# Two experts' second weights in column halves instead of three, and five batches with their left output half first instead of six

## Chip, cores, metric

One core of a Trainium2 chip runs the whole kernel. The metric is the device time of one execution in microseconds; the kernel before takes 181.04 us, the median of three runs (180.8 to 181.2).

## What is computed

Attention over 8 batches, 8 heads, 576 positions of 64 values (a sliding window of 32 for four heads, a dilated one for the other four), followed by a soft mixture of eight experts with four slots each. The change lies in the second part. With `x` the attention output as 4608 rows of 512:

```python
logits = x @ phi                                  # 4608 x 32
d = exp(logits - logits.max(0)); d /= d.sum(0)    # over the rows
slot_input = (d.T @ x).reshape(8, 4, 512)
for e in range(8):
    h = np.maximum(slot_input[e] @ w1[e], 0.0)    # 4 x 1024
    slot_out[e] = h @ w2[e]                       # 4 x 512
c = exp(logits - logits.max(1)); c /= c.sum(1)    # over the slots
return c @ slot_out.reshape(32, 512)              # 4608 x 512, float32
```

Every weight is read once: `w1` and `w2` have 2 MB for each expert in float32, and are held in float16 (1 MB).

## The kernel before

The attention is a software pipeline over the eight batches, in an order of steps written out by hand (`ORDER`, `STEPS`); the whole program is scheduled in the order in which it is written. All large transfers are issued by POOL, the inputs and weights (which are cast to float16 on the way) as well as the output, and so stand in one order. POOL issues the inputs of each batch, then the `w1` of the experts between them, then the `w2` of 0 to 2 (`load_w2`, L202).

Once the last inputs are consumed, their memory is released and takes the `w2` of experts 3 to 7 (L555 to L566). Experts 3 and 4 come whole, one transfer each of 8 KB per partition (L205). Experts 5, 6 and 7 come in column halves: first the left 256 output columns of 5, 6 and 7, then the right ones. A half is two transfers (L211, `u` 0 and 1), each of four rows of 256 columns per partition, so four transfers make an expert; the prediction calls such a transfer a quarter.

After the attention, PE computes the first layer for all experts (L616), the result is transposed into `hTm`, and `emit_so(s, experts)` (L641) multiplies with `w2` for the column half `s`, accumulating all eight experts in `so[s]`, one PSUM bank for each half. `gather_so` (L658) brings a half to SBUF as float16, `spread_so` (L662) sums its four row groups and copies the sum to all of them, in `so_sb`.

`emit_batch(b, c0, c1)` (L689) makes 512 output rows for the columns `c0` to `c1`: four times `emit_fin` (L670), a matmul into one of four PSUM buffers and a scaling by ACT (L681) or DVE (L685) in turn, and then one store by POOL (L692). A store of 256 columns has 512 KB, one of 512 columns 1 MB. The last 64 rows of each batch go through `om_l` and two stores at the end (L721).

The order at the end is thus: left half of the experts' product, the left half of the output of batches 0 to 5 (`NHALF`), with the right half of the experts 5, 6 and 7 multiplied ahead of batches 2, 3 and 5; then gather and spread of the right half, the right half of the output of batches 0 to 5, batches 6 and 7 whole, and the rest rows. PE, ACT, DVE and POOL each follow this order; the semaphores between them are set by which tile an instruction reads or writes. A store needs the scalings of its batch; the quarter that an `emit_so` reads must have landed.

Of the kernel before, what the change touches and what calls it, by code (L numbers as in the profile page):

```python
# [95 lines left out]
def kernel(  # L96
# [55 lines left out]
    def slab_weights(e, tag, n):  # L152
        t = fix.tile([128, n], FP16, name=f"w2_{e}", tag=tag)
        w2t[e] = t[:, 0 : 8 * DMODEL].rearrange("p (c n) -> p c n", c=8)
# [47 lines left out]
    def load_w2(e, s=None):  # L202
        src = moe_w2[e].rearrange("(p c) n -> p c n", p=128)
        if s is None:
            nc.gpsimd.dma_start(  # L205
                out=w2t[e].rearrange("p c n -> p (c n)"), in_=src.rearrange("p c n -> p (c n)")
            )
            return
        cols = slice(DH * s, DH * s + DH)
        for u in range(2):  # L210
            nc.gpsimd.dma_start(out=w2t[e][:, 4 * u : 4 * u + 4, cols], in_=src[:, 4 * u : 4 * u + 4, cols])  # L211
# [284 lines left out]
    def step(op, b):  # L496
        if op[0] in "ARM" and op[1:] in TILES:
            kind, i = TILES[op[1:]]
            if op[0] == "A":
                tmp[(op[1:], b)] = emit_av(b, kind, i)  # L500
            elif op[0] == "R":
                tmp[("R" + op[1:], b)] = emit_recip(b, kind, i, tmp[(op[1:], b)])
            else:
                engine = nc.scalar if op[1:] in ON_ACT else nc.vector
                norm_mult(b, kind, i, tmp.pop((op[1:], b)), tmp.pop(("R" + op[1:], b)), engine)
        elif op in ("S0", "S1", "S2"):
            tmp[(op, b)] = emit_scores(b, int(op[1]))
        elif op in ("E0", "E1", "E2"):
            emit_exp(b, int(op[1]), tmp.pop(("S" + op[1], b)))
        elif op in ("MK0", "MK1", "MK2"):  # L510
            emit_mask(b, int(op[2]))
        elif op[0:2] in ("QT", "KT", "VT"):
            turn(op[0], b, int(op[2]))
        elif op in ("XP0", "XP1"):
            tmp[(op, b)] = xT_plain(b, int(op[2]))
        elif op in ("XD0", "XD1"):
            tmp[(op, b)] = xT_dil(b, int(op[2]))
        elif op in ("XPc0", "XPc1", "XDc0", "XDc1"):
            xT_copy(b, op[1], int(op[3]), tmp.pop((op[0:2] + op[3], b)))
        elif op in ("VA", "VB", "VC", "VD"):  # L520
            tmp[(op, b)] = v_rows(b, "ABCD".index(op[1]))
        elif op in ("VAc", "VBc", "VCc", "VDc"):
            v_place(b, "ABCD".index(op[1]), tmp.pop((op[0:2], b)))
        elif op in ("LG", "EP"):
            tmp[(op, b)] = (back_logits if op == "LG" else back_erow)(b)
        elif op == "ET":
            back_et(b, tmp.pop(("LG", b)))
        elif op == "ER":
            back_er(b, tmp.pop(("EP", b)))
        else:  # L530
            {"ED": back_erd, "U": back_u, "UT": back_add}[op](b)

    def loads(which, b):
        load_raw(which, b)
        if which == "V":
            if b > 2:
                load_weights(1)
            if b == B - 1:
                load_weights(len(weights))
# [6 lines left out]
    for it in range(B + max(s for _, s in STEPS)):  # L546
        for op, stage in STEPS:
            b = it - stage
            if not 0 <= b < B:
                continue  # L550
            step(op, b)
            if op in frees and b + 2 < B:
                loads(frees[op], b + 2)
            left.discard((op, b))
            if w2b_pool is None and not left:  # L555
                raw_pool.release()
                w2b_pool = tc.alloc_tile_pool(name="w2b", bufs=1, side="right")
                for e in (3, 4, 5):
                    w2t[e] = w2b_pool.tile([128, 8, DMODEL], FP16, name=f"w2_{e}", tag=f"w2_{e}")
                slab_weights(6, "qk0", QK_SLAB)  # L560
                slab_weights(7, "qk1", QK_SLAB)
                for e in (3, 4):
                    load_w2(e)
                for s in range(2):
                    for e in (5, 6, 7):
                        load_w2(e, s)  # L566
        if it == 0:
            nc.vector.tensor_copy(
                out=phi4, in_=phi_raw[:, :, None, :].broadcast_to([128, 4, 4, N_SLOTS])
            )  # L570
# [40 lines left out]
    for fc in range(2):  # L611
        for g in range(2):
            for dc in range(4):
                for j in range(4):
                    e = 4 * g + j
# [25 lines left out]
    def emit_so(s, experts):  # L641
        for c in range(8):
            for e in experts:
                g, j = divmod(e, 4)
                row = 32 * (j if len(experts) == 4 else c % 4)
                nc.tensor.matmul(
                    so[s][row : row + 32, :],
                    hTm[:, g, c, 32 * j : 32 * j + 32],
                    w2t[e][:, c, DH * s : DH * s + DH],
                    start=(e < 4 and c == 0),  # L650
                    stop=(e == 7 and c > 3),
                )
# [5 lines left out]
    def gather_so(s):  # L658
        for copy, c, c0 in part_cols(s):
            copy(out=so_part[:, c0 : c0 + DH // 2], in_=so[s][:, c : c + DH // 2])  # L660

    def spread_so(s):  # L662
        for copy, _, c0 in part_cols(s):
            rep = ring.tile([128, DH // 2], FP32, name=f"rep_{c0}", tag="ring")
            nc.tensor.matmul(rep, spread, so_part[:, c0 : c0 + DH // 2], start=True, stop=True)
            copy(out=so_sb[:, c0 : c0 + DH // 2], in_=rep)
# [22 lines left out]
    def emit_batch(b, c0, c1):  # L689
        for j in range(4):  # L690
            emit_fin(et_cols(b)[0], j, c0, c1, om[b][:, j, c0:c1], 4 * b + j)
        nc.gpsimd.dma_start(  # L692
            out=out[S * b : S * b + 512].rearrange("(j p) d -> p j d", p=128)[:, :, c0:c1],
            in_=om[b][:, :, c0:c1],
        )

    NHALF = 6
    for s in range(2):
        emit_so(s, (0, 1, 2, 3))
    for s in range(2):  # L700
        emit_so(s, (4,))
    for e in (5, 6, 7):
        emit_so(0, (e,))
    gather_so(0)
    spread_so(0)
    for b in range(NHALF):
        if b in (2, 3, 5):
            emit_so(1, ({2: 5, 3: 6, 5: 7}[b],))
        if b == 5:
            gather_so(1)  # L710
        emit_batch(b, 0, DH)
    spread_so(1)
    for b in range(NHALF):
        emit_batch(b, DH, DMODEL)
    for b in range(NHALF, B):
        emit_batch(b, 0, DMODEL)
# [43 lines left out]
```

## Time and profile before

| | us |
|---|---|
| median of three runs | 181.04 (180.8 to 181.2) |
| the profiled execution | 180.9 |
| its span, first to last instruction | 178.9 |
| PE busy | 128.0 (72%) |
| DVE busy | 125.7 (70%) |
| ACT busy | 122.2 (68%) |
| POOL busy | 56.2 (31%) |
| moved by DMA | 40.88 MB, mean 229 GB/s |

The profile counts the bytes as they arrive: float16 for inputs and weights, float32 for the output. So the weights and the output, at the same number of elements, count as one and two. Every instruction has its start and length, every transfer its issue, its packets and its landings: it raises its semaphore once for each of the 16 transfer engines that it is spread over. Times below are counted from the start of the span.

### The profile page before, as it was taken

What the parts mean: (1) busy time and instruction counts of PE and PEld (TensorE: products, weight loads), DVE (VectorE), ACT (ScalarE), POOL (GpSimd) and SP (SyncE); (2) the same over time, 40 slices, a digit from 0 to 9 for tenths busy, and PEclk for the clock granted to TensorE, in tenths of its full rate; (3) what the DMA queues carried; (4) which work ended last, traced back from release to release, by engine and by line L of the source; (5) the groups of instructions that cost most, each with busy time, mean ns of one, the idle gap of its engine ahead of it and who ended that gap; (6) DMA issues with size and microseconds to landing.
All of it is one profiled execution on the core that took longest, in us unless ns stands there. A gap on an engine that the chain in (4) does not pass through costs nothing.

```text
span 178.9 us, 5405 instructions
## 1 busy us (share of the span) xinstructions
PE 128.0 (72%) x2316; PEld 84.7 (47%) x2316; DVE 125.7 (70%) x274; ACT 122.2 (68%) x267; POOL 56.2 (31%) x94
## 2 busy tenths in 40 slices
PE   0026838989999999989989999988695346688100
PEld 0014525676667767657767757856434112221000
DVE  6483999999999999999999995472402016789200
ACT  6007757999999999999999999966002016698100
POOL 7544244224224223243420041111112414376400
PEclk9999999999999879999999999687669955555555
DMA  5999999999999999999999999999999999999994
GB/s 91 203 213 208 214 212 210 214 212 216 214 212 213 215 212 215 214 212 216 210 214 215 212 218 220 215 216 220 211 212 191 197 196 219 390 319 397 406 413 135
DMA packets 21448, 40.88 MB, mean 229 GB/s; under 512 B 1713, under 2 KB 14129, under 8 KB 20785
## 3 DMA queue, kind: packets, MB, share of 16 engines
q0 software_dynamic: 21280, 40.41, 114.2%
q8 instruction: 18, 0.29, 0.6%
q1 hardware_dynamic: 144, 0.14, 0.3%
q14 instruction: 6, 0.04, 0.1%
HBM read 62.07 MB, written 9.44 MB: 400 GB/s over the span
## 4 chain that ended last, share of the span: by engine, by line
DMA 52%; DVE 16%; PE 11%; ACT 9%; issue 3%; POOL 2%; POOLq 0%; DVEq 0%
DMA w<-in_moe_w_dram 36%; DMA rawV<-in_v_dram 10%; DMA rawK<-in_k_dram 6%; DVE vT L222 5%; DVE qk L222 4%; DVE p L283 3%; PE f L672 3%; ACT p L272 3%; ACT om L681 2%; PE s L263 2%; PE o_P L313 2%; PE rv L237 2%; ACT xp L337 1%; PE rp L357 1%; ACT vX L243 1%
## 5 line engine op out<-in xcount | busy, mean ns | idle before, releaser
L272 ACT ACTIVATE p<-s 128x1728 f16<-128x1728 f32 (+1 forms) x24 | 42.0, 1749 | 10.7 <-PE s L263 10.6
L263 PE MATMUL s<-qk 32*128 32x144 f16 (+2 forms) x640 | 29.2, 325 | 16.1 <-DVE qk L222 12.3
L313 PEld LDWEIGHTS <-p 128*128 128x128 f16 (+3 forms) x672 | 23.9, 101 | 14.0 <-issue 3.6
L263 PEld LDWEIGHTS <-qk 32*128 32x128 f16 x640 | 17.0, 118 | 20.4 <-DVE qk L222 12.3
L337 ACT ACTIVATE xp<-o_P,rc_P 128x64 f16<-128x64 f32 x96 | 23.8, 384 | 2.4 <-DVE rc_P L325 2.3
L283 DVE TENSOR_TENSOR p<-p,masks 128x1728 f16<-128x1728 f16 (+1 forms) x24 | 25.4, 1082 | 0.0
L243 ACT COPY vX<-rv 128x512 f16<-128x512 f16 (+1 forms) x32 | 23.5, 786 | 1.7 <-PE rv L237 1.6
L313 PE MATMUL o_P<-vX,p 128*128 128x65 f16 (+1 forms) x288 | 20.7, 210 | 1.3 <-DVE xp L341 0.3
L222 DVE STREAM_TRANSPOSE qk<-rawQ 128x576 uint32<-128x576 uint32 x16 | 18.9, 1243 | 2.7 <-DMA rawQ<-in_q_dram 2.7
L222 DVE STREAM_TRANSPOSE qk<-rawK 128x576 uint32<-128x576 uint32 x16 | 19.7, 1241 | 0.5 <-DMA rawK<-in_k_dram 0.5
L222 DVE STREAM_TRANSPOSE vT<-rawV 128x576 uint32<-128x576 uint32 x16 | 19.6, 1238 | 0.4 <-DMA rawV<-in_v_dram 0.4
L237 PE MATMUL rv<-cst,vT 128*128 128x128 f16 x160 | 17.3, 248 | 3.0 <-DVE vT L222 1.7
L211 POOL DMA_DIRECT2D w<-in_moe_w_dram x12 | 8.9, 745 | 29.1 <-DMA w<-in_moe_w_dram 24.8
L685 DVE TENSOR_SCALAR om<-f,rrow 128x256 f16<-128x256 f32 (+1 forms) x28 | 13.5, 518 | 3.9 <-PE f L672 3.1
L237 PEld LDWEIGHTS <-vT 128*128 128x128 f16 x160 | 12.0, 127 | 8.6 <-issue 4.3
L191 POOL DMA_DIRECT2D rawQ<-in_q_dram x16 | 8.9, 557 | 21.5 <-DVE rc_P L325 16.3
L681 ACT ACTIVATE om<-f,rrow 128x256 f16<-128x256 f32 (+1 forms) x28 | 12.8, 503 | 3.3 <-PE f L672 2.6
L672 PE MATMUL f<-so_sb,ET 32*128 32x256 f16 (+1 forms) x60 | 12.1, 420 | 3.7 <-ACT om L681 2.4
L692 POOL DMA_DIRECT2D out_dram<-om x14 | 10.4, 747 | 12.1 <-DVE om L685 9.4
L191 POOL DMA_DIRECT2D rawK<-in_k_dram x16 | 8.7, 548 | 17.1 <-DVE rc_P L325 14.6
L191 POOL DMA_DIRECT2D rawV<-in_v_dram x16 | 8.7, 547 | 10.8 <-DVE rc_P L325 8.0
L372 ACT COPY xT<-rp 128x576 f16<-128x576 f16 x16 | 10.5, 776 | 1.2 <-PE rp L357 1.2
(84 smaller groups left out, 197.4 us busy)
## 6 DMA issues: line engine op xcount, KB each, us to landing
w<-in_moe_w_dram POOLq DMA_DIRECT2D x13, 1024.0 KB, 21.7
out_dram<-om POOLq DMA_DIRECT2D x12, 512.0 KB, 6.2
rawQ<-in_q_dram POOLq DMA_DIRECT2D x16, 288.0 KB, 10.7
rawK<-in_k_dram POOLq DMA_DIRECT2D x16, 288.0 KB, 10.4
rawV<-in_v_dram POOLq DMA_DIRECT2D x16, 288.0 KB, 10.2
w<-in_moe_w_dram POOLq DMA_DIRECT2D x12, 256.0 KB, 16.4
out_dram<-om POOLq DMA_DIRECT2D x2, 1024.0 KB, 8.6
out_dram<-om_l POOLq DMA_DIRECT2D x2, 512.0 KB, 9.1
```

The source lines that it names most:

```text
L191: nc.gpsimd.dma_start(out=t[g::2, :], in_=src[4 * g : 4 * g + 4].rearrange("h (p j) d -> (h p) (j d)", j=PJ),)
L222: nc.vector.transpose(out=out_, in_=in_)
L237: nc.tensor.transpose(rg[:, n_t, :, c, :], rows, ident)
L243: copy(out=vX[b % 2][:, t0 : t0 + n, :, 0:D], in_=rg.rearrange("p n h c d -> p n h (c d)"))
L263: nc.tensor.matmul(sps[:, h, c0 : c0 + w], kk, qq, start=(tt == 0), stop=(tt == 1))
L272: return nc.scalar.activation(out=pt, in_=sps[:, :, 0:n], func=AF.Exp, scale=SCALE)
L283: return nc.vector.tensor_tensor(out=pt, in0=pt, in1=m, op=ALU.mult)
L313: nc.tensor.matmul(o[rows, h, :], lhs, rhs, start=(n == 0 or (kind == "L" and n < DIL)), stop=(n == len(jobs) - 1), skip_group_check=True,)
L337: nc.scalar.activation(out=dst[:, h], in_=src[:, h], func=AF.Copy, scale=rc[:, h : h + 1])
L672: nc.tensor.matmul(fp[:, 0 : c1 - c0], ET[32 * j : 32 * j + 32, m : m + 128], so_sb[32 * j : 32 * j + 32, c0:c1], start=True, stop=True,)
L681: nc.scalar.activation(out=dst, in_=fp[:, 0 : c1 - c0], func=AF.Copy, scale=rrow[:, blk : blk + 1])
L685: nc.vector.tensor_scalar(out=dst, in0=fp[:, 0 : c1 - c0], scalar1=rrow[:, blk : blk + 1], scalar2=None, op0=ALU.mult)
```

## The change

Expert 5's `w2` comes whole, behind those of 3 and 4, and only 6 and 7 come in column halves. Both halves of expert 5's product are multiplied ahead of the left halves of 6 and 7. Five batches instead of six have the left half of their output first; the right half of expert 6 is multiplied ahead of batch 2's left half, that of expert 7 ahead of batch 4's, and the gather of the right half follows it there. Batch 5 is then made whole, like 6 and 7.

```diff
-                for e in (3, 4):
+                for e in (3, 4, 5):
                     load_w2(e)
                 for s in range(2):
-                    for e in (5, 6, 7):
+                    for e in (6, 7):
                         load_w2(e, s)
...
-    NHALF = 6
-    for s in range(2):
-        emit_so(s, (0, 1, 2, 3))
-    for s in range(2):
-        emit_so(s, (4,))
-    for e in (5, 6, 7):
+    NHALF = 5
+    for experts in ((0, 1, 2, 3), (4,), (5,)):
+        for s in range(2):
+            emit_so(s, experts)
+    for e in (6, 7):
         emit_so(0, (e,))
     gather_so(0)
     spread_so(0)
     for b in range(NHALF):
-        if b in (2, 3, 5):
-            emit_so(1, ({2: 5, 3: 6, 5: 7}[b],))
-        if b == 5:
+        if b in (2, 4):
+            emit_so(1, (5 + b // 2,))
+        if b == NHALF - 1:
             gather_so(1)
         emit_batch(b, 0, DH)
     spread_so(1)
```

## The prediction

> **What bounds the kernel now.** I read the slices of the page first, since they show whether the transfers ever rest.
>
> ```profile
> DMA  5999999999999999999999999999999999999994
> GB/s 91 203 213 208 214 212 210 214 212 216 214 212 213 215 212 215 214 212 216 210 214 215 212 218 220 215 216 220 211 212 191 197 196 219 390 319 397 406 413 135
> q0 software_dynamic: 21280, 40.41, 114.2%
> ```
>
> The 16 transfer engines are busy from the first slice to the last but one. Two places stand out: 191 to 197 GB/s in slices 31 to 33, where w2 comes in halves, and 319 between 390 and 397 in slice 36, in the middle of the output. Nearly all of it goes through one queue, q0, fed by POOL. So I asked for windows (columns: window, length, busy of PE, PEld, DVE, ACT, POOL, clock, DMA share, GB/s).
>
> ```profile
> 112.00:132.00 20.00, 16.68 (x294) 11.90 (x290) 8.10 (x31) 10.47 (x28) 2.97 (x4) 0.68 1.03 216
> 137.00:150.00 13.00, 6.90 (x126) 3.73 (x126) 2.33 (x6) 2.80 (x7) 4.40 (x6) 0.74 1.45 196
> 150.00:151.00 1.00, 0.45 (x12) 0.14 (x8) 0.88 (x2) 0.84 (x2) 0.81 (x2) 0.50 1.22 186
> 157.00:159.00 2.00, 1.71 (x9) 0.48 (x9) 1.55 (x4) 1.83 (x5) 1.39 (x2) 0.50 1.08 214
> 159.00:176.00 17.00, 6.16 (x23) 1.14 (x20) 7.24 (x13) 6.33 (x12) 6.57 (x10) 0.50 1.73 401
> ```
>
> Whole w2 comes at 216 GB/s, halves at 196; output leaves at 401, but at 214 in 157 to 159. What POOL did around that hole is in its timeline:
>
> ```profile
> 143.36 0.74 POOL L211 DMA_DIRECT2D w<-in_moe_w_dram  x1 [1.44 <-DMA w<-in_moe_w_dram]
> 149.31 0.75 POOL L692 DMA_DIRECT2D out_dram<-om  x1 [5.21 <-DVE om L685]
> 150.24 0.75 POOL L692 DMA_DIRECT2D out_dram<-om  x1 [0.18 <-issue]
> 151.51 0.75 POOL L692 DMA_DIRECT2D out_dram<-om  x1 [0.52 <-DVE om L685]
> 153.19 0.75 POOL L692 DMA_DIRECT2D out_dram<-om  x1 [0.94 <-ACT om L681]
> 154.14 0.75 POOL L692 DMA_DIRECT2D out_dram<-om  x1 [0.20 <-issue]
> 157.61 2.96 POOL L692 DMA_DIRECT2D out_dram<-om  x4 [2.73 <-DVE om L685]
> ```
>
> Five left halves go out by 154.14, the sixth only at 157.61. Its rows were scaled by 155.40; other stores start 0.5 us after their last scaling, so this one lost some 1.7 us to something that the profile does not name.
>
> The landing records settle who pays. Each transfer counts its semaphore up 16 times, once per engine, and the counts spread: w2_4 lands from 134.06 to 136.87, the last quarter of w2 from 150.10 to 153.58. Eight engines are early, eight late (152.25 and after), the last two at 152.92 and 153.58. The only packets that go to single engines are the PE's 16 KB instruction reads (18, about 0.95 us each); the one at 140.66 moved one engine from 140.90 to 143.08 in place of 1.34 us, the one at 153.96 another by 0.7. In the hole the early engines run dry and the last two do not: they land outputs every 1.25 to 1.4 us throughout and finish at 177.10 and 177.39, the others by 176.46. The span is 177.39 + 1.5. So the bound is the latest engine's own work, and the hole costs it nothing.
>
> **The change part by part.** Expert 5's w2 becomes one load in place of four quarters. On the first engine a quarter takes (150.10 - 134.06) / 12 = 1.337 us, a whole load 134.06 - 129.19 = 4.87. Saved: 4 x 1.337 - 4.87 = 0.48 us on every engine.
>
> Here a page bears. The Trainium skill (DMA: Bandwidth & Descriptors, Anatomy of one DMA) gives about 2.0 us plus bytes for each transfer; as an estimate that is 3 x 2.0 = 6 us saved. The trace disagrees: queued transfers overlap, and four quarters cost 0.48 more.
>
> Batch 5 leaves whole. Two half stores take 2 x 1.322 us (160.62 to 168.55 on the first engine is six), a whole one 2.54 to 2.59 (168.55, 171.09, 173.68): 0.07 saved. Four matmuls and four scalings of 256 columns become halves of longer ones (0.48 each against 0.69 to 0.75 for 512 columns), hidden under 23 us of queued output. POOL issues 86 transfers in place of 90, at 0.74 us, each after the eighth before it has landed (its waits name eight semaphores in turn). The last quarter can now issue once w2_5 has landed, at 142, some 9 us before its turn, and the first store waits for 6's first quarter, long there: nothing.
>
> The weights end therefore on the latest engine at 153.58 - 0.47 = 153.11.
>
> But expert 5's right half now stands ahead of the left halves of 6 and 7. The last left quarter landed at 145.60, 8.73 after w2_4. Now: 4.87 + 4 x 1.34 + the 0.70 of the instruction read, which PE's position puts in the same place, = 10.93, so 147.80: 2.2 later. From that landing to the first store's issue (matmul, gather, spread, four scalings) it was 149.31 - 145.60 = 3.71, all one after the other and unchanged. First store: 151.5.
>
> An idle engine lands a half store 3.0 us after its issue (149.31 to 152.31; again 157.61 to 160.62); a busy one 1.32 to 1.39 after its previous landing. So first landing: 154.5 on all 16. The latest engine, free at 153.11, would reach 153.11 + 1.39 = 154.5 anyway and loses nothing; the second latest, free at 152.4, loses 0.7; the early eight, free at 149.6, lose over 3, where they lost 0.7 before. The skew that shielded the critical engine is spent: all begin the output level.
>
> From 154.5 on, each engine has 9 half stores after the first (11.9), 3 whole (7.7), 2 of om_l (1.20 + 1.25): 176.55. The engine that gets the instruction read of 153.96 adds 0.7 to 0.95; PE reaches the same rows at 154 to 156, after output has begun, so it is not absorbed. I take 0.75, between its own jump (0.68) and its later lead over the level engines (0.85): 177.3, against 177.39.
>
> The supply has to hold for that: a store must be issued 1.65 us before the engine's previous landing. Batches take 0.95 us, 1.27 with a part of right half between (rows of before): issues 151.5, 152.4, 153.7, 154.6. The wait of so(1) for 7 ends at 153.1, now behind batch 3, whose scalings run to 154.1; PE then does its 8 matmuls (0.6), and gather, batch 4 and spread follow, with the fin matmuls of batch 0's right half queued behind them. Batch 4 goes at 156.1 (needed by 156.85), batch 0's right half at 157.6 (158.2), then one each 0.96 against 1.32. Margins are 0.5 to 0.75 us.
>
> Then the 1.7 us pause. No row says what it is; it may vanish (0) or stay 1.7 or so. Where it falls decides: after batch 3's right half there is 2 us of slack (ready 161.45, needed by 163.45), so there it is hidden; at batch 4's left half it is not. I take hidden: the transfer eight before it had landed at 150.95 and its rows were done, so it waited on nothing of its place; and the left half's own gather and spread (146.1 to 147.3) put no pause ahead of the first store.
>
> A rule speaks to that. The Trainium skill says that the descriptor rings lie in 16 KiB per partition (SBUF — State Buffer, SBUF size) and that a descriptor has 16 bytes (DMA: Bandwidth & Descriptors, Why small descriptors are slow): an estimate of 1024 per ring. The trace agrees so far: q0's 21280 packets are 1330 per engine, 999 of them before the sixth left half, which takes 33. By that rule the pause is the ring's turn, and the change moves it to batch 4's right half (1008 before it).
>
> Sum: 177.3 - 177.39 = -0.1: 180.8 on the profiled execution's 180.9, and 180.9 on the median, which is 0.14 above it.
>
> **The rivals.** *Faster: only the work counts.* If the second instruction read falls before the output starts, or the left half is ready by 150.8, no engine waits longer and the savings stay: -0.48 - 0.07, 180.4 to 180.5. For it: the critical engine itself loses nothing. Against: the second latest is made to wait. 0.24.
>
> *Slower: the pause stays at the last left store.* It followed the gather and spread of the right half; if these bring it, batch 4 goes at 156.1 + 1.7 = 157.8 where 156.85 was needed. All engines land it at 160.8, and 7.7 + 6.6 + 2.45 remain: 177.6, or 178.3 if the instruction read falls after it. So +0.2 to +0.9, middle 181.6. It decides once batch 4's store is issued after 157. For it: one pause only, at that place. Against: the casts of that spread had ended by 155.6, two us earlier. 0.18.
>
> *Slower: the left half is later still.* Should the second instruction read also hit the engine that lands 7's left last, the first store goes at 152.3 and every 0.1 beyond 151.5 is paid by all 16 engines: +0.7, 181.7. It decides at a first issue after 152. Against: in before, that read came 8 us after that landing. 0.14.
>
> **How the numbers follow.** About 0.2% (0.36 us) is what can be told from no change. My own case, -0.1 with some 0.3 for supply and landings on either side, has 0.44 and stays within it; the faster rival has 0.24, the two slower ones 0.32 together. The range runs from the faster case's 180.4 less 0.2 to the slower cases' 181.9.
>
> **What would show it.** Right: w2_5 lands about 141.7, the last left quarter 147.8, the last weights 153.1; first L692 at 151.5; GB/s near 130 or less for 1 to 2 us before the output, no hole of half rate at the last left half; early and late engines within 1 us through the output. Wrong: a gap of over 1.5 us on POOL ahead of batch 4's left half, output slices well under 390, or a first store before 151 or after 152.

## The result, and the profile after

The changed kernel takes 181.93 us (median of six runs, 181.61 to 182.41), the kernel before 181.0 in the same rounds (180.8 to 181.2). The ratio is 1.0045, with an interval of 1.0034 to 1.0056: slower by 0.9 us. The forecast was 180.9, no change. The profiled execution of after took 181.79 us, its span is 180.0. Its last store landed at 178.72 and that of before at 177.39, with 1.3 and 1.5 us of the span behind it. These 1.33 us are what has to be explained.

From the page of after, the slices and the queue:

```profile
GB/s 95 209 212 209 214 210 212 213 216 214 214 212 211 214 211 217 212 213 217 211 212 216 214 216 221 217 217 215 215 217 206 193 196 97 395 396 369 418 414 105
q0 software_dynamic: 18784, 40.41, 111.1%
```

Slice 36, in the middle of the output, has risen from 319 to 396 (slice 37 now has 369); the one ahead of the output, slice 34, has fallen from 219 to 97. The same windows of after as those shown of before (window, length, busy of PE, PEld, DVE, ACT, POOL, clock, DMA share, GB/s):

```profile
112.00:132.00 20.00, 15.99 (x330) 11.61 (x331) 8.11 (x31) 11.16 (x32) 2.97 (x4) 0.80 1.03 216
137.00:150.00 13.00, 5.98 (x126) 3.94 (x127) 1.01 (x3) 1.12 (x3) 1.43 (x2) 0.80 1.31 193
150.00:151.00 1.00, 0.47 (x7) 0.21 (x3) 0.79 (x2) 0.84 (x2) 0.00 (x0) 0.50 0.74 100
157.00:159.00 2.00, 1.71 (x9) 0.48 (x7) 1.56 (x4) 1.82 (x5) 1.07 (x2) 0.50 1.99 400
159.00:176.00 17.00, 6.90 (x25) 1.35 (x22) 7.94 (x13) 6.97 (x13) 6.13 (x9) 0.50 1.66 400
```

The hole of 157 to 159 is filled (400 in place of 214). Instead, from 150 to 151 the transfers move 100: the early engines have run out of weights (the first lands its last ones at 149.54) and no store has been issued. Finer, in steps of 0.5 us from 145 to 165 (the DMA view of after for that stretch):

```profile
GB/s 193 198 199 193 198 196 195 196 183 130 100 99 95 32 12 23 395 410 385 420 379 371 397 387 410 397 387 406 391 395 399 385 408 395 389 397 387 408 401 268
```

The 10th to 16th values, 149.5 to 153, are the empty stretch. From 153 on all engines leave output at full rate together. POOL's timeline of after, at the places that the prediction named:

```profile
141.77 0.74 POOL L211 DMA_DIRECT2D w<-in_moe_w_dram  x1 [4.08 <-DMA w<-in_moe_w_dram]
151.65 0.75 POOL L692 DMA_DIRECT2D out_dram<-om  x1 [9.14 <-DVE om L685]
...
156.10 0.75 POOL L692 DMA_DIRECT2D out_dram<-om  x1 [0.55 <-ACT so_sb L666]
157.73 0.74 POOL L692 DMA_DIRECT2D out_dram<-om  x1 [0.89 <-ACT om L681]
...
161.06 0.74 POOL L692 DMA_DIRECT2D out_dram<-om  x1 [0.22 <-ACT om L681]
163.83 2.22 POOL L692 DMA_DIRECT2D out_dram<-om  x3 [2.03 <-ACT om L681]
```

The first store goes at 151.65, batch 4's at 156.10, batch 0's right half at 157.73, all within 0.15 of the forecast. The pause stands ahead of the tenth store, which is issued at 163.83, the ninth at 161.06. So the order of events came out as foreseen, and still the end is 1.3 us late. The landing records, one per engine and sorted within each transfer, show where (us):

```
                       before                        after
last w2 quarter        150.10 ... 152.92 153.58      149.54 ... 152.17 153.30
first store            152.31 ... 154.29 154.97      154.64 ... 154.95 155.05
second store           153.64 ... 156.30 156.65      156.00 ... 156.22 158.07
last store             176.13 ... 177.10 177.39      176.95 ... 177.26 178.72
```

In after 15 engines stay together through the whole output, and one leaves the pack between the first and the second store: from 155.05, the latest landing of the first, to 158.07 it is 3.02 us, for a step that takes the others 1.31. It never catches up: it ends 1.46 us behind the next one. A 16 KB instruction read of PE starts at 154.99, where that step begins.

### The profile page after: what moved, and what is told of

It is laid out like the page before. It is cut to its first block, busy times and chain, and to the rows that moved or that the text cites. A ratio compares the mean times of both kernels' runs of the same rounds, so it can differ in the third digit from the quotient of the medians.

```text
span 180.0 us, 5388 instructions
## 1 busy us (share of the span) xinstructions
PE 128.5 (71%) x2312; PEld 85.6 (48%) x2312; DVE 125.4 (70%) x272; ACT 121.9 (68%) x265; POOL 53.0 (29%) x90
## 4 chain that ended last, share of the span: by engine, by line
DMA 43%; PE 18%; ACT 17%; DVE 11%; issue 3%; POOL 2%; POOLq 0%; DVEq 0%; ACTq 0%
DMA w<-in_moe_w_dram 32%; DMA rawK<-in_k_dram 7%; ACT p L272 6%; PE s L263 5%; DMA rawV<-in_v_dram 5%; PE f L672 4%; DVE qk L222 3%; PE rv L237 3%; ACT om L681 3%; DVE vT L222 3%; ACT xp L337 2%; ACT vX L243 2%; ACT xT L374 2%; ACT xT L372 1%; DVE p L283 1%
## 5 line engine op out<-in xcount | busy, mean ns | idle before, releaser
L313 PEld LDWEIGHTS <-p 128*128 128x128 f16 (+3 forms) x672 | 24.4, 102 | 14.1 <-issue 4.0
L337 ACT ACTIVATE xp<-o_P,rc_P 128x64 f16<-128x64 f32 x96 | 24.3, 407 | 2.6 <-DVE rc_P L325 2.6
L237 PE MATMUL rv<-cst,vT 128*128 128x128 f16 x160 | 18.4, 261 | 2.9 <-DVE vT L222 1.8
L237 PEld LDWEIGHTS <-vT 128*128 128x128 f16 x160 | 12.6, 131 | 8.5 <-issue 4.3
L211 POOL DMA_DIRECT2D w<-in_moe_w_dram x8 | 5.9, 743 | 28.9 <-DMA w<-in_moe_w_dram 28.6
L692 POOL DMA_DIRECT2D out_dram<-om x13 | 9.7, 745 | 15.2 <-DVE om L685 9.7
```

The costliest lines, as they stand in the source:

```text
L237: nc.tensor.transpose(rg[:, n_t, :, c, :], rows, ident)
L313: nc.tensor.matmul(o[rows, h, :], lhs, rhs, start=(n == 0 or (kind == "L" and n < DIL)), stop=(n == len(jobs) - 1), skip_group_check=True,)
L337: nc.scalar.activation(out=dst[:, h], in_=src[:, h], func=AF.Copy, scale=rc[:, h : h + 1])
```

## The experiments

Three theories stood at the start. **A**: expert 5's right half stands ahead of the left halves of 6 and 7, so the first store is late and all engines begin the output level. **B**: five batches instead of six, with the POOL pause at its new place, cost the time. **C**: the instruction read delays one engine by more than I had charged, and hurts only because that engine no longer has a lead. Below, the engines are called skewed when the 16 landings of one transfer lie far apart (3.48 us for the last weights of before) and level when they lie close together (0.41 for the first store of after). Each ratio is to the kernel before, run beside it (181.1 to 181.15 us).

**The two halves of the change, one at a time.** `order_only` is the kernel before with the new order of loads, still in quarters and with six batches:

```diff
-                for s in range(2):
-                    for e in (5, 6, 7):
-                        load_w2(e, s)
+                for e, s in ((5, 0), (5, 1), (6, 0), (7, 0), (6, 1), (7, 1)):
+                    load_w2(e, s)
```

> The kernel before with one thing of the change: expert 5's right half is loaded ahead of the left halves of 6 and 7, still in quarters; six batches keep their left half first. Theory A (the change loses because the left half of the product, and with it the first output store, comes later than the transfer engines finish w2): the last left quarter lands at about 148.6 instead of 145.6, the first store is issued at about 152.3 instead of 149.3, the engines stand idle before it, and the run takes 182.2 to 182.6, somewhat more than the changed kernel, since nothing is saved on packets. Theory B (it loses because fewer batches have their left half first, which moves POOL's pause to a place without cover): 181.0, as before.

`five_batches` is the kernel before with its loads, and five batches:

```diff
-    NHALF = 6
+    NHALF = 5
...
-        if b in (2, 3, 5):
-            emit_so(1, ({2: 5, 3: 6, 5: 7}[b],))
-        if b == 5:
+        if b in (2, 3, 4):
+            emit_so(1, (3 + b,))
+        if b == NHALF - 1:
```

> The kernel before with the other thing of the change: five batches have their left half first, batch 5 is made whole; the loads stay as they were (5, 6 and 7 in halves, all left halves first). Theory A (late first store): first store at 149.3 as before, 181.0 to 181.3. Theory B (fewer left halves and the moved pause cost it): 181.7 to 182.0. By the count of descriptors POOL's pause (999 descriptors per engine before the sixth store) should stand before the sixth store, which is now the right half of batch 0.

And `six_batches` is the changed kernel with its loads, and six batches:

```diff
-    NHALF = 5
+    NHALF = 6
...
-        if b in (2, 4):
-            emit_so(1, (5 + b // 2,))
+        if b in (2, 5):
+            emit_so(1, ({2: 6, 5: 7}[b],))
```

> The changed kernel with six batches' left halves first again, loads as changed (5 whole, only 6 and 7 in halves); the right half of 6 is multiplied ahead of batch 2, that of 7 ahead of batch 5. Theory A (the late first store): first store at about 151.7 as in the changed kernel and the run as slow, 181.8 to 182.1. Theory B (number of batches): 181.1. By the descriptor count (909 per engine through the sixth left half, 33 each after it) POOL's pause should stand before the right half of batch 3.

Measured: order_only 181.95 us, ratio 1.0057 (1.0036 to 1.0078); five_batches 181.29, 1.0008 (0.9993 to 1.0024); six_batches 182.28, 1.0063 (1.0043 to 1.0083). The window of 149 to 153 separates them; first order_only, then five_batches (a fence for each):

```profile
149.00:153.00 4.00, 3.08 (x30) 0.90 (x29) 2.48 (x7) 2.56 (x8) 1.06 (x2) 0.50 0.78 105
```

```profile
149.00:153.00 4.00, 3.11 (x32) 0.93 (x31) 2.89 (x7) 2.65 (x7) 2.25 (x3) 0.50 1.45 240
```

With the new order of loads 105 GB/s (after: 84), with the old order 240 (before: 263). Both kernels with the new order are slow, the one with five batches alone is not. B falls as the cause. In order_only and six_batches, too, one engine leaves the pack; the last ends 1.2 and 1.5 us behind the first (last store 177.48 to 178.69, and 177.40 to 178.93). order_only came out a little below what A had forecast (first store issued at 151.76, not 152.3), six_batches a little above. So A is needed for the loss, but these runs do not say whether it suffices: all have an instruction read in the output.

**The left half made early.** `left_without_67` is the changed kernel whose left half leaves out the product of experts 6 and 7, and so no longer waits for them:

```diff
-                    stop=(e == 7 and c > 3),
+                    stop=(e == (5, 7)[s] and c > 3),
...
-    for e in (6, 7):
-        emit_so(0, (e,))
```

> The changed kernel, but the left half of the experts' product leaves out experts 6 and 7 (their left quarters are loaded all the same, so the transfers are the same and in the same order); the left half can be gathered as soon as expert 5 has landed. Theory A: first store issued at about 145.5 to 146, queued behind w2, no engine idle before the output; the latest engine ends 1.3 to 1.7 us earlier than in the changed kernel: 180.2 to 180.6. Theory B: the batches and the pause are those of the changed kernel: 181.9.

Measured: 180.14 us, 0.9933 (0.9912 to 0.9953). First store issued at 146.36, landed between 150.95 and 154.77. The read comes at 156.0 here, also in the output; the last store lands from 176.43 to 177.20. With the skew between engines back (3.82 us at the first store, 1.47 at the third, which lands as the read starts) the read costs little: these landings are 0.77 apart, where those of after are 1.77 apart.

**Less PE work.** In `wide` experts 0 to 5 are multiplied for all 512 columns at once (one PSUM bank for both halves), 48 matmuls fewer for the same sums. Its core:

```diff
-        for s in range(2):
-            emit_so(s, experts)
+        emit_so_whole(experts)
...
+    def emit_so_whole(experts):
+        for c in range(8):
+            for e in experts:
...
+                nc.tensor.matmul(
+                    so_all[row : row + 32, :],
+                    hTm[:, g, c, 32 * j : 32 * j + 32],
+                    w2t[e][:, c, :],
...
```

> The changed kernel with 48 matmuls fewer: experts 0 to 5, whose w2 comes whole, are multiplied with all 512 columns at once, both halves of the product in one PSUM bank. Theory C (the time is set by one transfer engine that the PE's last instruction read falls on, at PE instruction 4553 of 4627): PE has 4531 instructions, the read may not come at all, the latest engine then ends with the others, 1.3 to 1.6 us earlier: 180.3 to 180.6, under both kernels. If the read is not tied to that position it comes all the same, and the run takes 181.8 to 182.0. Theory A alone, without C, gives 181.9 too, since the first store is not earlier by more than 0.1.

Measured: 180.47 us, 0.9972 (0.9947 to 0.9997), faster than both. The first store is no earlier (issued 151.77, landed 154.78 to 155.14); but the last PE read now comes at 180.6, when all is done, and the last store lands on all engines between 177.15 and 177.52. Three of its twelve executions, the profiled one among them, have 1 to 1.5 us more outside the span than the others (181.6 with a span of 178.8).

`short_after` and `short_before` leave out, in seven of the eight batches, the part of the last 64 rows that comes from the dilated tiles. That takes 224 PE instructions out of the attention, in the changed kernel and in the one before, with the same edit:

```diff
-            elif kind == "L":
+            elif kind == "L" and b == B - 1:
```

> The changed kernel with 224 PE instructions fewer, all in the attention: seven of the eight batches leave out the part of the last 64 rows that comes from the dilated tiles. The transfers are the same. Theory C (the read of PE's instructions that falls into the output is paid in full): with this length the last read falls elsewhere or away, as in the kernel with 512 columns at once, the 16 engines end within 0.5 us of each other, 180.3 to 180.6. If a read still falls into the output: 181.8 to 182.1.

> The kernel before with the same 224 PE instructions left out. Theory C: without a read in the output the engine that was latest gains no more than 0.3, since the one hit by the read before it follows 0.3 behind: 180.7 to 180.9, so that the change alone would then be 0.2 to 0.4 faster where it was 0.9 slower. If the change's loss is the late first store whatever the reads do (theory A without C): before stays 0.8 to 0.9 faster than the changed kernel of the same length.

Measured: short_after 180.00 us, 0.9942 (0.9924 to 0.9960); short_before 180.79, 0.9984 (0.9971 to 0.9998). short_after is 0.3 faster than expected. The last reads fall at 151.96, in the empty stretch, and at 151.60, among the last weights of short_before, whose first output lands at 151.56 on the engines that are ahead. The last store lands from 176.35 to 177.10 and from 176.35 to 177.19. The pair is the comparison of the change with no read that delays the output: 0.8 us faster, where with the read in the output it is 0.9 slower.

**More PE work.** Less work could itself have been the gain. So the next three do more: `long_after` and `long_before` compute the product of experts 0 to 3 with their left columns twice, the first pass being overwritten (32 matmuls more, ahead of PE's waits for w2); `longer_after` does so for both halves (64 more).

```diff
+                    skip_group_check=True,
...
+    emit_so(0, (0, 1, 2, 3))
     NHALF = 5
```

> The changed kernel with 32 matmuls more and nothing less: the product of experts 0 to 3 with their left columns is computed twice (the first pass is overwritten). They run at about 138 us, some 0.5 us of PE time, while PE has waits of several us for w2 behind them. The sequencer then stands 64 instructions further when it comes to the same place in the output, so that the read of 154.99 should fall where PE stood 64 instructions earlier, at about 150 us, ahead of the first store. By the read (theory C): no 16 KB read in the output, the last store lands on all engines within 0.8 us, at about 177.0 to 177.5, and the time is 180.2 to 180.8, with more work faster than the changed kernel by 0.6% or more. By the rival, that wide and short_after were faster since PE had less to do: not faster than the changed kernel, 181.9 or more.

> The same with 64 matmuls more (both halves of the product of experts 0 to 3 computed twice), some 1 us of PE time, also ahead of waits for w2. By the read (theory C): the read that stood at 154.99 now falls where PE stood 128 instructions earlier, at about 142 us, among the loads of w2; 180.2 to 180.8, unless a later read has moved into the output. By the rival (less PE work was the gain): 181.9 or more.

> The kernel before with the same 32 matmuls more. The read of 153.96 should fall at about 150 us, during the last loads of w2. By the read (theory C): the kernel before paid it out of the lead of one engine, so little is to be gained: 180.6 to 181.1, the last store landing 176.4 to 177.3. By the rival: 181.0 to 181.5.

Measured: long_after 180.58 us, 0.9967 (0.9953 to 0.9982); longer_after 180.52, 0.9972 (0.9957 to 0.9988); long_before 181.09, 1.0004 (0.9991 to 1.0017). The changed kernel becomes 1.35 us faster by doing more; the slowest of the twelve executions of long_after (181.39) is faster than the fastest of after (181.61). The reads moved to 148.90, 151.29 and 149.71. The place expected for longer_after, about 142, was wrong; 151.29 lies in its empty stretch, so that its time came out as expected. The DMA view for the stretch from 152 to 178 has q8, which carries PE's instructions, in after and no longer in long_after (queue, packets, MB, share); first after, then long_after:

```profile
q0 software_dynamic: 7429, 9.44, 157.9%
q8 instruction: 1, 0.02, 0.2%
```

```profile
q0 software_dynamic: 7465, 9.47, 158.3%
```

The empty stretch is still there in long_after:

```profile
149.00:153.00 4.00, 2.62 (x23) 0.99 (x23) 2.68 (x7) 2.69 (x7) 1.33 (x2) 0.50 0.75 106
```

Its first store goes at 151.49 and lands level (154.48 to 154.88), its pause is 2.03 us ahead of the tenth store as in after, and yet its last store lands at 176.79 to 177.15. So neither the late first store nor the level start nor the pause makes the kernel slower than before. The read does, and only with the level start (median times, us):

| | read in the output | no read in it |
|---|---|---|
| engines skewed (loads of before) | before 181.0; five_batches 181.29 | long_before 181.09 |
| engines level (loads of after) | after 181.93; order_only 181.95; six_batches 182.28 | long_after 180.58; longer_after 180.52; wide 180.47 |

**A smaller whole part.** `wide_half5` is wide with only half of expert 5's rows whole and the other half in columns, to get the left half earlier and keep some of the saving:

```diff
-                for e in (3, 4, 5):
+                for e in (3, 4):
                     load_w2(e)
+                load_w2(5, "top")
                 for s in range(2):
+                    load_w2(5, s, (1,))
                     for e in (6, 7):
...
```

> A version meant to beat both: the kernel with 512 columns at once, but with a half of expert 5's rows (512 KB) in column halves again, so that the right quarter of it stands behind the left halves of 6 and 7; the left half of the product should be ready 1.0 us earlier, first store at 150.7 to 150.9 instead of 151.8. Theory A: the eight late engines no longer wait, the latest engine is bound by its own work (w2 ends at 153.7 on it): ends at 177.1, 180.0 to 180.2 against 180.5. If only the count of bytes and packets matters: 0.24 slower than that kernel, 180.7.

Measured: 182.13 us, 1.0067 (1.0046 to 1.0088); the expectation failed. Its first store goes at 150.67, a read comes at 164.5, in the output, and the pause has moved forward to the eighth store, in POOL's timeline of wide_half5:

```profile
158.68 0.74 POOL L716 DMA_DIRECT2D out_dram<-om  x1 [0.20 <-ACT om L705]
161.90 2.96 POOL L716 DMA_DIRECT2D out_dram<-om  x4 [2.48 <-DVE om L709]
```

There the supply is not ahead enough: on the first engine the next landing takes 2.84 us (162.07 to 164.91) in place of 1.32, and the last engine goes from 163.02 to 166.61. I had moved two things of which I knew only that they move.

## Why the prediction was wrong

**What held.** The saving of whole loads (w2_5 landed 141.48, forecast 141.7; the last weights 153.30, forecast 153.11), the delay of the left half (last left quarter 147.94, forecast 147.8), the first store (151.65, forecast 151.5), its level landing (154.64 to 155.05, forecast 154.5), the read falling behind the start of the output (154.99, forecast 154 to 156), the supply after it and the place of the pause.

**The step that failed** is the term for the instruction read: "The engine that gets the instruction read of 153.96 adds 0.7 to 0.95 [...] I take 0.75". It was mis-sized: the engine that was hit paid about 2.0 us, and 1.7 at the least. I had the 0.7 from matching ranks in sorted landings (154.29 to 156.30 and so on), as if the last but one before were the last but one after. Ranks change when one engine is delayed. In before the engine at 154.97 gives the 156.30 one step later (1.33), and the 156.65 belongs to an engine that had been further ahead. A measure without ranks is the step of the mean of the 16 landings from first to second store, less the same step where no read falls into it, times 16. In before it is 16 x (1.417 - 1.32) = 1.5 us (1.32 and 1.33 in short_before and long_before), in after 16 x (1.415 - 1.29) = 2.0 (1.285 to 1.296 in wide, short_after, longer_after and long_after). The least is what remains if the engine's own first landing was the latest: 3.02 - 1.31 = 1.7.

The same error stands in the prediction's reading of the read at 140.66: 140.90 to 143.08 in place of 1.34 makes 0.84, the mean 16 x (1.411 - 1.335) = 1.2. For the last left quarter the error was hidden by luck: in after the read of 141.98 made the latest landing later by 147.94 - 141.48 - 4 x 1.34 = 1.1 in place of 0.70, and w2_5 had landed 0.2 earlier than forecast. The profile also has five smaller instruction packets (q14 of the page), which the prediction did not count; the last comes at 104.7, far ahead of the output.

By the sums, the engine that was hit in before had landed its first store at about 156.65 - 1.32 - 1.5 = 153.8 (an estimate): 1.1 us ahead of the latest. It paid 1.1 of its 1.5 out of this lead. The prediction said that the change spends the skew "that shielded the critical engine"; it shielded the engine that the read hits, and I did not charge for that.

From 177.3 forecast to 178.72 measured it is 1.42. At the second store it had been 1.50: 158.07, where 154.5 + 1.32 + 0.75 = 156.57 follows from the forecast. About 1.25 of that is the read (2.0 instead of 0.75) and about 0.25 the engine's first landing; with the least for the read it is 0.95 and 0.55. 0.15 of the landing is the later issue. For the other engines, forecast 176.55 and measured 176.95, it is 0.15 for the store and 0.3 for the pause, below.

**The rivals.** The faster rival had named its own condition: "If the second instruction read falls before the output starts [...] the savings stay", 180.4 to 180.5. long_after, with that condition made true, measures 180.58, longer_after 180.52. So the mechanism was right and the condition was false for the kernel as it is. The first slower rival (the pause stays at the last left store) did not occur: batch 4's store left at 156.10. The second (first issue after 152) did not either, though its time, 181.7, is near. My own case with the read at 1.7 to 2.0 gives 181.85 to 182.15, and 181.93 was measured.

**The pause.** It was forecast as hidden. Nearly: ahead of the tenth store of after the other engines take 1.62 in place of 1.32, so 0.3 us, while the latest, 167.29 to 168.62, lost nothing. The rule by which its place was given (the Trainium skill, SBUF — State Buffer, SBUF size, and DMA: Bandwidth & Descriptors, Why small descriptors are slow, an estimate of 1024 descriptors per ring) agrees with all 13 traces: the pause stands ahead of the store with which the count per engine passes from 999 or 1008 to 1032 or 1041, whichever store that is. As 79 or 80 transfers stand ahead of it in each, a count of transfers is not excluded; that was not tested.

**What stays open.** Which engine a read goes to, and at which instruction PE asks for it: when the read inside the output started, PE stood anywhere from 11 (wide_half5) to 102 (order_only) matmuls and weight loads ahead of its last; 64 instructions more moved the read of after 6 us forward, 128 more only 3.7. Why a packet of about 0.95 us delays the engine's queue by 1.0 to 2.0 us, differently in each kernel, is not shown either. Nor do the traces, one for each kernel, show where the read fell in the other executions.

## What to carry to other kernels

A sum for the engine that ends last holds only if nothing else reaches an engine that had been ahead: when a change takes away the skew between the transfer engines, every delay of a single engine that was paid out of a lead is paid in full. Before judging a small difference in a kernel bound by its transfers, look where the instruction reads of the busiest engine fall, and shift them by a few dozen instructions that cost nothing; here that was worth 1.35 us, more than the change itself. Where a shifted read ends up has to be read from the new trace. Do not follow engines through sorted landings by rank: take sums over all 16.

## What the hardware showed

- PE's instructions arrive in 16 KB packets through the same 16 transfer engines as the data: 18 in a run, 17 in the two kernels with 224 PE instructions fewer, most of them about 0.95 us long. One of them held one engine's data back by 1.0 us in five_batches (16 x (1.392 - 1.33)), 1.5 in before, 1.6 in order_only (16 x (1.391 - 1.29)) and about 2.0 in after. The Trainium skill (Runtime: NRT & Kernel Launch, Instruction fetch mechanics) describes refills of 16 KiB that the sequencer fetches while it executes, and calls their cost "mostly hidden". The size agrees; in this queue of data the cost is not hidden: 181.93 us with the read in the output, 180.58 with it ahead.
- POOL idles for 2.0 to 3.6 us ahead of one store in every run, at the place that the descriptor count gives, where 0.2 to 0.9 is usual between stores that need no more weights. It cost the latest engine of before nothing, the other 15 engines of after 0.3 us, and most engines of wide_half5 1.5.
- The same edit was measured at -0.4% (short_after against short_before) and at +0.45% (after against before), by where PE's reads fall.
